# Four rows of a modulation made together in 32-column quarters of TensorE and spread over the partitions through DRAM

## The chip, the cores and the metric

The kernel runs on one core of a Trainium2 chip. A core has TensorE (PE, matrix products from SBUF into PSUM), VectorE (DVE), ScalarE (ACT), GpSimd (POOL) and SyncE (SP, which here issues nearly all DMA transfers). Every engine works through its own list of instructions in order and waits for others through semaphores. The metric is the device time of one execution in microseconds, the median of several.

## The reference

A block of a network, forward and backward, on 2048 rows of 512 values in bf16; the hidden width F is 1792. A vector `c` makes six modulation rows; two sublayers follow, a spectral filter and an MLP with squared ReLU. The outputs are the block's result and the gradients by x, the filter's two parts, w1, b1, w2, b2, c and w_mod.

```python
mod = (_silu(c) @ w_mod).reshape(c.shape[0], 6, 1, -1)
sa, ca, ga, sb, cb, gb = (mod[:, 0].copy(), ..., mod[:, 5].copy())
h = _layernorm(x, axis=-1) * (1 + ca) + sa
x = x + ga * _A_ref(h, A_w_r, A_w_i)      # irfft2(rfft2(h) * (w_r + i w_i))
h = _layernorm(x, axis=-1) * (1 + cb) + sb
x = x + gb * _B_ref(h, B_w1, B_b1, B_w2, B_b2)   # relu(h w1 + b1)**2 w2 + b2
```

## The kernel before

The kernel is written out instruction by instruction, and then `set_order` puts each engine's instructions into the order of a table, `ORDER`: a list of positions for each of the five engines. Tiles and buffers are given out by pools; who waits for whom follows from the data.

The stage of this change is the start, some 55 us. Four things run in it side by side:

- x is loaded (`x_sb`), its rows get their statistics on DVE (`row_stats`), are normalized (`row_norm`, whose result also goes to `n_dram`), multiplied by 1 + ca (L833) and folded (`fold_u`, L277 and L278). On the folded rows PE does the first half of the two-dimensional transform (L313, L314, into `psA`).
- PE multiplies the incoming gradient (transposed, `gT`) with the transposed w2, scaled by 2 gb (`w2T`, L892): work that fills PE wherever the rest waits.
- DVE and ACT make tables of sines and cosines (L245 to L256 and others).
- The six modulation rows are made. `mod_row(j)` multiplies silu(c), repeated over all 128 columns (`scb`), with a 512 x 512 block of w_mod: four 128x512 matmuls (L772) into `mod_ps`, of which there is one buffer, with the same row on all partitions as the result. ACT or DVE copies it to `modb` (L774 to L778). Row 5 is also made as a column, by sixteen 128x1 matmuls (L787), since w2T is scaled by it. Row 0 goes to `srow` (L781, L782), is turned into columns by four matmuls with `pm` (L864, `sacol`), and adds a constant to the transform (L871, `dcrow`, L350). Rows 3 and 4 (sb and 1 + cb) are turned into columns by eight matmuls (L876) that read `modb`; the result `mcol` is used much later (L1039, L1041).

Then `spec_f23` begins, the second half of the transform: eight groups of `psB` matmuls on PE, each emptied by ACT into `AE` (L359). Its first `psB` needs all folded rows and `dcrow`; the mcol matmuls stand right behind it on PE.

In the end stage the gradient of w2 is made in 14 chunks of 128 rows of F (`grad_w2`, L1441). Each chunk needs a transposed load from `h_dram` (`hn`, issued on SP at L1257), sixteen 128x512 matmuls (for chunks 10 and 13 two halves of sixteen 128x256), a copy on ACT (L1442) and a store (L1443). Buffers `hn` are used again, so a load waits for the last matmul of an earlier chunk.

## Time and profile before

| | us |
|---|---|
| timed runs, three: median | 394.21 |
| their lowest and highest | 394.0 and 395.75 |
| the profiled execution's own span, first to last instruction | 398.0 |
| PE busy in it | 382.1 |
| DVE, ACT, POOL busy in it | 334.8, 303.2, 33.3 |

For the profiled execution no time is given but its span, which is 3.8 us above the median of the timed ones. Its mean granted TensorE clock is 0.990 of full speed. Busy times are sums over stages with different limits; each stage has to be looked at by itself.

### The profile page before, as it was taken

How to read it: one execution, taken by the hardware profiler on the slowest of the kernel's cores; microseconds unless marked ns; L12 is line 12 of the kernel's file. 1: busy time of each engine (PE TensorE's matmuls, PEld its weight loads, DVE VectorE, ACT ScalarE, POOL GpSimd, SP SyncE). 2: the span in 40 equal slices, each digit the busy share in tenths (PEclk: the TensorE clock that was granted, in tenths of full speed). 3: DMA queues.
4: the chain of work that ended last, by engine and by line, in shares of the span. 5: the costliest groups of instructions: out<-in, count | busy, mean ns of one | idle time of the engine just before them, and what ended most of it. 6: DMA issues, size and time to landing. Idle time of an engine off the chain costs nothing.

```text
span 398.0 us, 8415 instructions
## 1 busy us (share of the span) xinstructions
PE 382.1 (96%) x3042; PEld 202.4 (51%) x3042; DVE 334.8 (84%) x822; ACT 303.2 (76%) x605; POOL 33.3 (8%) x114
## 2 busy tenths in 40 slices
PE   8999999999999999999999999999999999999495
PEld 3555677544444444444444435457666664444244
DVE  8899959949986699969997999957999989998430
ACT  4787899899896499759976999277665589998441
POOL 9151001000000000000000000012300000002100
PEclk9999999999999999999999999999999999999979
DMA  8999799874589999578928696999979998999995
GB/s 258 362 222 293 230 209 252 209 280 63 195 228 197 256 259 253 128 191 183 257 81 210 167 245 180 270 245 371 296 221 262 215 325 173 221 208 243 249 259 189
DMA packets 133957, 91.06 MB, mean 229 GB/s; under 512 B 86842, under 2 KB 119868, under 8 KB 133660
## 3 DMA queue, kind: packets, MB, share of 16 engines
q1 hardware_dynamic: 132904, 88.09, 87.1%
q0 software_dynamic: 832, 2.36, 1.8%
q8 instruction: 24, 0.39, 0.4%
q14 instruction: 17, 0.14, 0.1%
q10 hardware_dynamic: 180, 0.07, 0.1%
HBM read 38.70 MB, written 33.19 MB: 181 GB/s over the span
## 4 chain that ended last, share of the span: by engine, by line
PE 74%; ACT 12%; DMA 5%; DVE 4%; POOL 2%; issue 1%; SPq 0%; ACTq 0%; POOLq 0%; DVEq 0%
PE og_1s L1096 12%; PE og_0s L1096 11%; PE mm_0s L1441 6%; PE mm_1s L1441 6%; PE mm_0s L1342 5%; PE mm_1s L1342 5%; PE mm_1s L1064 4%; PE mm_0s L1064 4%; PE pst L1064 3%; DMA hn_1s<-h_dram 3%; PE mm_0s L892 2%; DMA Xb<-xs_dram 2%; ACT AE L359 2%; PE mm_1s L892 2%; ACT gab L896 2%; ACT gab L1073 1%
## 5 line engine op out<-in xcount | busy, mean ns | idle before, releaser
L1342 PEld LDWEIGHTS <-h_sb 128*64 128x64 bf16 (+1 forms) x464 | 28.7, 109 | 15.9 <-issue 0.9
L1073 ACT ACTIVATE gab<-gab 128x512 bf16<-128x512 bf16 x56 | 35.0, 648 | 0.5 <-DVE gab L1071 0.5
L1096 PEld LDWEIGHTS <-gab 128*128 128x128 bf16 x224 | 21.5, 98 | 27.0 <-ACT gab L1073 1.9
L1064 PEld LDWEIGHTS <-w 128*128 128x128 bf16 x224 | 21.2, 98 | 25.7 <-issue 1.7
L1342 PE MATMUL mm_0s<-gab,h_sb 128*64 128x384 bf16 (+2 forms) x288 | 32.7, 345 | 0.0
L892 PEld LDWEIGHTS <-w2T 128*128 128x128 bf16 (+1 forms) x280 | 22.9, 102 | 18.5 <-issue 3.9
L1096 PE MATMUL og_0s<-w1T,gab 128*128 128x512 bf16 x112 | 27.4, 379 | 0.2 <-ACT G_0s L1109 0.2
L1096 PE MATMUL og_1s<-w1T,gab 128*128 128x512 bf16 x112 | 27.6, 379 | 0.0
L1441 PE MATMUL mm_0s<-g_sb,hn_1s 128*128 128x512 bf16 x64 | 16.8, 423 | 6.0 <-DMA hn_1s<-h_dram 6.0
L1342 PE MATMUL mm_1s<-gab,h_sb 128*64 128x512 bf16 (+2 forms) x176 | 22.4, 370 | 0.0
L1064 PE MATMUL mm_1s<-h2T,w 128*128 128x512 bf16 x84 | 21.9, 379 | 0.0
L1064 PE MATMUL mm_0s<-h2T,w 128*128 128x512 bf16 x80 | 21.2, 379 | 0.0
L359 ACT ACTIVATE AE<-psB 128x1024 bf16<-128x1024 f32 x16 | 17.2, 1078 | 0.7 <-PE psB L355 0.6
L896 ACT CAST gab<-mm_1s 128x512 bf16<-128x512 f32 x24 | 14.8, 615 | 2.3 <-PE mm_1s L892 2.2
L892 PE MATMUL mm_0s<-gT_0s,w2T 128*64 128x512 bf16 (+1 forms) x76 | 16.1, 380 | 0.2 <-DVE gab L894 0.2
L892 PE MATMUL mm_1s<-gT_0s,w2T 128*128 128x512 bf16 (+1 forms) x72 | 15.6, 379 | 0.1
L1064 PE MATMUL pst<-h2T,w 128*128 128x512 bf16 x60 | 15.6, 379 | 0.0
L892 PE MATMUL mm_1s<-gT_1s,w2T 128*128 128x512 bf16 (+1 forms) x68 | 14.9, 379 | 0.3 <-ACT gab L896 0.2
L892 PE MATMUL mm_0s<-gT_1s,w2T 128*128 128x512 bf16 (+1 forms) x64 | 15.1, 379 | 0.0
L1441 PEld LDWEIGHTS <-hn_1s 128*128 128x128 bf16 x64 | 6.8, 107 | 15.3 <-DMA hn_1s<-h_dram 6.2
L321 POOL MEMSET AE<- 128x4 bf16 x4 | 0.4, 110 | 162.4 <-PE mm_1s L1064 162.4
L1441 PE MATMUL mm_1s<-g_sb,hn_0s 128*128 128x512 bf16 (+1 forms) x64 | 13.7, 352 | 0.0
(650 smaller groups left out, 1064.3 us busy)
## 6 DMA issues: line engine op xcount, KB each, us to landing
w<-in_B_w_dram SPq DMA_DIRECT2D x2, 1792.0 KB, 10.4
Xb<-xs_dram SPq DMA_DIRECT2D x4, 514.0 KB, 7.9
Z<-wz_dram SPq DMA_DIRECT2D x4, 514.0 KB, 7.5
x_sb<-in_A_x_dram SPq DMA_DIRECT2D x4, 512.0 KB, 6.2
n_dram<-x_sb SPq DMA_DIRECT2D x4, 512.0 KB, 6.2
h_dram<-h2r SPq DMA_DIRECT2D x8, 256.0 KB, 2.4
h_sb<-h_dram SPq DMA_DIRECT2D x4, 512.0 KB, 5.4
g_sb<-in_grad_out_dram SPq DMA_DIRECT2D x2, 1024.0 KB
```

The costliest lines, as they stand in the source:

```text
L321: nc.gpsimd.memset(ae[:, :, :, 256:257], 0.0)
L359: nc.scalar.activation(dst, ps.rearrange("p r b (e f) -> p (r b) f e", e=2), AF.Copy, scale=EF_S)
L892: nc.tensor.matmul(ps[m], lhsT=w2T[:, dc, fc * P + m.start:fc * P + m.stop], rhs=gT[b][:, :, dc, :], start=(dc == 0), stop=(dc == 3), **pos)
L896: nc.scalar.copy(out=gaT[b][:, fc, :], in_=ps)
L1064: nc.tensor.matmul(ps, lhsT=w1[:, dc, (fc + i) * P:(fc + i + 1) * P], rhs=h2T[b][:, :, dc, :], start=(dc == 0), stop=(dc == 3))
L1073: nc.scalar.activation(gh[:, i, :], gh[:, i, :], AF.Copy, accum_out=gb1[:, b, fc + i:fc + i + 1])
L1096: nc.tensor.matmul(ps, lhsT=lhs(fc), rhs=rhs[:, fc, :], start=(fc == 0), stop=(fc == NFC - 1))
L1342: nc.tensor.matmul(blocks(ps[m], fb), lhsT=h2_sb[:, t, dc * P + m.start:dc * P + m.stop], rhs=gh_rows(t, fb), start=(t == 0), stop=(t == N ...
L1441: nc.tensor.matmul(ps[:, 0:w], lhsT=hns[fc][:, t, :], rhs=g_sb[:, t, c:c + w], start=(t == 0), stop=(t == NT - 1))
```

## The change

`mod_row` becomes `mod_rows`. For one row (j = 1) it does what was done before. For the four rows 2, 5, 4, 3 it gives each row a quarter of TensorE's columns: the weight is 32 columns of the repeated silu(c), the result 32 partitions of `mod_ps`. One ACT instruction copies all four with a bias `one4`, which is 1 on the partitions of row 4 and 0 elsewhere. One row of each quarter is stored to the new `mod_dram` (4 x 512 values, 4 KB), and a second DMA reads them back into `modb` on all 128 partitions (512 KB); `modb` has its rows in another order for that. `mod_cols` is the old form of row 5, and now also makes row 0, straight as columns. Where row 0 was reversed on the copy to `srow`, two of its columns are now reversed by a matmul with a mirrored identity (`flip`). The table `ORDER` is new for all engines; of its lines one is shown.

```diff
 ORDER = {
     "PE": (
-        "0-7 30 8-13 31 14-16 52-59 17-22 32-47 23-26 64-67 27 60-63 28 76-83 29 68-75 89-93 237-240 84-88 99-103 241-242 245-246 "
+        "0-1 3 5 2 4 6 8 7 30 9 11 13 10 15 12 17 14 16 31 19 21 32-47 18 56-59 52-55 20 22-23 64-67 60-63 24 26 25 76-83 27 "
...
+    mod_dram = dram.tile([4, D], BF16, name="mod_dram")
...
-    GA_B, GB_B, CA1_B, CB1_B, SB_B = range(5)
+    GA_B, GB_B, CB1_B, SB_B, CA1_B = range(5)
...
-    srow = gall[:, 1, :]
-
-    def mod_row(j):
+    one4 = constp.tile([P, 1], FP32, name="one4")
+    nc.gpsimd.memset(one4, 0.0)
+    nc.gpsimd.memset(one4[64:96, :], 1.0)
+
+    def mod_rows(*js):
         ps = psM.tile([P, D], FP32, name="mod_ps", bufs=1)
+        if len(js) == 1:
+            for dc in range(4):
+                nc.tensor.matmul(ps, lhsT=scb[:, dc, :], rhs=wmt[js[0] // 2][:, dc, (js[0] % 2) * D:(js[0] % 2 + 1) * D], start=(dc == 0), stop=(dc == 3))
+            nc.scalar.activation(modb[:, CA1_B, :], ps, AF.Identity, bias=K["onef"])
+            return
         for dc in range(4):
-            nc.tensor.matmul(ps, lhsT=scb[:, dc, :], rhs=wmt[j // 2][:, dc, (j % 2) * D:(j % 2 + 1) * D], start=(dc == 0), stop=(dc == 3))
...
+            for q, j in enumerate(js):
+                nc.tensor.matmul(ps[32 * q:32 * q + 32, :], lhsT=scb[:, dc, 32 * q:32 * q + 32], rhs=wmt[j // 2][:, dc, (j % 2) * D:(j % 2 + 1) * D],
+                                 start=(dc == 0), stop=(dc == 3), tile_position=(0, 32 * q))
+        row4 = gall[:, 1, :]
+        nc.scalar.activation(row4, ps, AF.Identity, bias=one4)
+        nc.sync.dma_start(mod_dram, row4[0:P:32, :])
+        nc.sync.dma_start(modb[:, 0:4, :], mod_dram[None, :, :].broadcast_to([P, 4, D]))
+
+    def mod_cols(j):
+        psc = psM.tile([P, 4], FP32, name="sm_ps", bufs=1)
+        for cc in range(4):
+            for dc in range(4):
+                a = (j % 2) * D + cc * P
+                w = wmt[j // 2][:, dc, a:a + P]
+                nc.tensor.matmul(psc[:, cc:cc + 1], lhsT=w, rhs=sc[:, dc:dc + 1], start=(dc == 0), stop=(dc == 3))
+        return psc
+
+    psc = mod_cols(5)
...
-    mod_row(1)
+    mod_rows(1)
...
-    for j in (0, 4, 3, 2, 5):
-        mod_row(j)
+    flip = p0.tile([P, P], BF16, name="flip")
+    nc.gpsimd.tensor_copy(flip, K["ident"][:, ::-1])
+    psc = mod_cols(0)
+    nc.vector.tensor_copy(sacol[:, 0, :], psc)
+    psc = psM.tile([P, 2], FP32, name="sm_ps", bufs=1)
+    nc.tensor.matmul(psc, lhsT=flip, rhs=sacol[:, 0, 1:4:2], start=True, stop=True)
+    nc.vector.tensor_copy(sacol[:, 0, 1:4:2], psc)
+    nc.vector.tensor_scalar(sacol[:, 1, :], sacol[:, 0, :], -1.0, None, op0=ALU.mult)
+    mod_rows(2, 5, 4, 3)
...
-    for i in range(4):
-        sr = srow[:, i * P:(i + 1) * P]
-        nc.tensor.matmul(psc[:, i, :], lhsT=sr, rhs=pm, start=True, stop=True)
-    nc.vector.tensor_copy(sacol[:, 0:2, :], psc[:, 0:4, :].rearrange("p i k -> p k i"))
```

What the new table does to the lists is seen at three places. The line numbers in rows of the changed kernel are its own: L788 is the quarter matmul, L792 and L793 the two DMAs, L895 the mcol matmuls (L876 before), L911 the w2 matmuls (L892), L848 the store to n_dram (L831), L871 the loads of Z (L854), L1276, L1460 and L1462 the `hn` load, the chunk's matmul and its store (L1257, L1441, L1443).

First, PE where modulation rows are made. Before, a row of four full matmuls (here row 5, in part) stands between first-stage matmuls, and the other rows stand at four more places:

```order
L314 LDWEIGHTS fold_u_1s
L314 MATMUL psA_0s<-TA,fold_u_1s 128x2x128
L772 LDWEIGHTS gab
L772 MATMUL mod_ps<-wm_2s,gab 128x512
L772 LDWEIGHTS gab
L772 MATMUL mod_ps<-wm_2s,gab 128x512
L772 LDWEIGHTS gab
L772 MATMUL mod_ps<-wm_2s,gab 128x512
L313 LDWEIGHTS fold_u_0s
L313 MATMUL psA_1s<-TA,fold_u_0s 128x2x128
```

In the changed kernel all sixteen quarter matmuls stand together, of which these are the first four (`wm_1s` and `wm_2s` are the blocks of w_mod for rows 2, 3 and 4, 5; `gab` holds the repeated silu(c)):

```order
L911 MATMUL mm_0s<-gT_1s,w2T 128x512
L788 LDWEIGHTS gab
L788 MATMUL mod_ps<-wm_1s,gab 32x512
L788 LDWEIGHTS gab
L788 MATMUL mod_ps<-wm_2s,gab 32x512
L788 LDWEIGHTS gab
L788 MATMUL mod_ps<-wm_2s,gab 32x512
L788 LDWEIGHTS gab
L788 MATMUL mod_ps<-wm_1s,gab 32x512
```

They are the 242nd to 257th of PE's matmuls; the first `psB` is the 330th, and the mcol matmuls stand from the 348th on.

Second, SP and PE along the way through DRAM. On SP the two new DMAs stand among loads of Z and stores of n_dram; what a row waits for is in brackets, and `DMAHW7_49` and the like are the landings of earlier DMAs (a DMA also waits for the one before it on its own of eight such marks):

```order
L1098 DMA wz_dram<-in_A_w_i_dram 32x7x257 [waits DMAHW5_49]
L871 DMA Z<-in_A_w_r_dram 64x2x257 [waits DMAHW6_49]
L792 DMA mod_dram<-gab 4x512 [waits DMAHW7_49,Activation_49]
L848 DMA n_dram<-x_sb 128x2x1024 [waits DMAHW0_49,DVE_49]
L848 DMA n_dram<-x_sb 128x2x1024 [waits DMAHW1_49]
L871 DMA Z<-in_A_w_i_dram 32x7x257 [waits DMAHW2_49]
L793 DMA modb<-mod_dram 128x2048 [waits DMAHW7_49,DMAHW3_49]
L871 DMA Z<-in_A_w_i_dram 32x7x257 [waits DMAHW4_49]
L848 DMA n_dram<-x_sb 128x2x1024 [waits DMAHW5_49,DVE_49]
```

and on PE the mcol matmuls, which before waited for copies of ACT and DVE, wait for the second of them:

```order
L355 MATMUL psB<-Cd,utcs 64x128
L895 LDWEIGHTS modb [waits DMAHW3_49]
L895 MATMUL sm_ps<-pm,modb 128x1
L895 LDWEIGHTS modb
L895 MATMUL sm_ps<-pm,modb 128x1
```

So the rows now leave PE, ACT, SP and two transfers behind them before PE goes on past `psB`.

Third, SP at the end, where the last four chunks' loads stand (chunk 10 is the first `hn` row in both, then 11, 12, 13). Before:

```order
L1257 DMA_TRANSPOSE hn_0s<-h_dram 128x16x128
L1334 DMA gxl_1s<-gx_dram 128x1024
L1257 DMA_TRANSPOSE hn_1s<-h_dram 128x16x128
L1443 DMA out_dram<-gw_2s 128x512
L1257 DMA_TRANSPOSE hn_2s<-h_dram 128x16x128
L481 DMA wmc_1s<-in_w_mod_dram 128x4x512
L1257 DMA_TRANSPOSE hn_3s<-h_dram 128x16x128
L1443 DMA out_dram<-gw_3s 128x512
L1443 DMA out_dram<-gw_4s 128x512
```

In the changed kernel, from the store of chunk 4 on (`gw_5s` and `gw_7s` are chunks 5 and 7):

```order
L1462 DMA out_dram<-gw_4s 128x512
L1334 DMA out_dram<-b4r_0s 1x512
L1462 DMA out_dram<-gw_5s 128x512
L1462 DMA out_dram<-gw_7s 128x512
L1276 DMA_TRANSPOSE hn_1s<-h_dram 128x16x128
L481 DMA wmc_1s<-in_w_mod_dram 128x4x512
L1276 DMA_TRANSPOSE hn_2s<-h_dram 128x16x128
L1276 DMA_TRANSPOSE hn_3s<-h_dram 128x16x128
L1353 DMA gxl_1s<-gx_dram 128x1024
```

The load of chunk 11 (`hn_1s`) has moved behind the stores of chunks 4, 5 and 7. PE takes the chunks in the order 5, 7, 6, 9, 8, 10 (first half), 11 in the changed kernel, with the last four of chunk 9 behind chunk 8; before it was 5, 6, 7, 8, 9, 10 (first half), 11.

## Rows read from the trace of the kernel before

**Rows 1.** The page: busy time, share of the span and instructions of each engine.

```profile
PE 382.1 (96%) x3042; PEld 202.4 (51%) x3042; DVE 334.8 (84%) x822; ACT 303.2 (76%) x605; POOL 33.3 (8%) x114
```

**Rows 2.** Table by stages: us, busy PE, PEld, DVE, ACT, POOL, clock, DMA.

```profile
36.00:55.00 19.00, 19.00 (x173) 11.90 (x172) 16.03 (x50) 16.04 (x28) 1.75 (x4) 1.00 0.93 228
55.00:75.00 20.00, 19.66 (x287) 13.49 (x283) 17.94 (x36) 19.27 (x34) 2.01 (x6) 1.00 0.89 237
```

**Rows 3.** The chain of work that ended last, 30 to 56: start, us, what.

```profile
43.38 0.86 PE mod_ps L772 x4
...
45.11 0.89 PE mod_ps L871 x16
46.11 0.11 PE psA_1s L314
...
50.34 0.23 PE psB L355 x4
...
51.01 0.29 PE sm_ps L876 x8
```

**Rows 4.** Timeline of DVE around the last fold: start, us, engine, line, what.

```profile
46.14 0.68 DVE L256 TENSOR_TENSOR LF<-lf_w_0s,lf_mk 128x256 bf16<-128x256 bf16 x3
...
47.08 0.41 DVE L278 TENSOR_TENSOR fold_u_1s<-h_1s 128x512 bf16<-128x512 bf16 x1
47.41 0.24 DVE L180 TENSOR_SCALAR Cf<-Cf,cf_f 128x128 bf16<-128x128 bf16 x1
```

**Rows 5.** Timeline of PE, the first matmul on the last fold.

```profile
47.57 0.27 PE L313 MATMUL psA_1s<-TA,fold_u_1s 128*128 128x256 bf16 x1
```

**Rows 6.** Waits of PE: line, waited for, us in total, times, longest.

```profile
PE mm_0s L1441 <- DMA hn_1s<-h_dram: 6.0, 1, 6.0
```

**Rows 7.** Timeline of SP's queue in the tail.

```profile
366.24 5.22 SPq L1257 DMA_TRANSPOSE hn_1s<-h_dram  x1
```

**Rows 8.** Timeline of PE in the tail.

```profile
371.03 1.36 PE L1441 MATMUL mm_1s<-g_sb,hn_0s 128*128 128x256 bf16 x11
378.36 5.97 PE L1441 MATMUL mm_0s<-g_sb,hn_1s 128*128 128x512 bf16 x16 [5.96 <-DMA hn_1s<-h_dram]
```

**Rows 9.** The chain of work in the tail.

```profile
384.33 3.45 PE mm_1s L1441 x16
```

**Rows 10.** Table by stages of 5 us in the tail, columns as above.

```profile
370.00:375.00 5.00, 2.40 (x17) 1.42 (x15) 3.99 (x10) 2.70 (x5) 1.60 (x3) 1.00 1.22 156
375.00:380.00 5.00, 1.64 (x4) 0.58 (x5) 0.00 (x0) 0.00 (x0) 0.00 (x0) 0.63 1.11 305
```

**Rows 11.** The chain of work, 149 to 152: matmuls with 32-column weights.

```profile
149.85 0.98 PE acc L959 x16
```

**Rows 12.** The chain of work, 9 to 12: row 5 made as columns.

```profile
10.52 0.38 PE sm_ps L787 x16
```

**Rows 13.** Lines 776 and 865: count, shortest, median and longest in ns, starts, forms.

```profile
L776 DVE TENSOR_SCALAR modb<-mod_ps x1: 682/682/682, 38.8 to 38.8; 128x512 bf16<-128x512 f32 x1
...
L865 DVE CAST sacol<-sm_ps x1: 167/167/167, 28.7 to 28.7; 128x8 bf16<-128x8 f32 x1
```

**Rows 14.** Line 778, the same columns.

```profile
L778 ACT CAST modb<-mod_ps x3: 585/585/585, 40.8 to 44.3; 128x512 bf16<-128x512 f32 x3
```

**Rows 15.** Line 831, the stores of n_dram, 512 KB each.

```profile
L831 SPq DMA_DIRECT2D n_dram<-x_sb x4: 360/372/383, 34.3 to 43.0; - x4
...
DMA to landing us min/median/max: 3.7/6.2/7.0
```

**Rows 16.** DMA issues: count, size, median us from issue to landing.

```profile
LF_dram<-LF SPq DMA_DIRECT2D x4, 256.0 KB, 4.0
...
out_dram<-gw_0s SPq DMA_DIRECT2D x2, 128.0 KB, 1.7
...
wz_dram<-in_A_w_i_dram SPq DMA_DIRECT2D x4, 112.4 KB, 7.8
```

**Rows 17.** The tile hn_1s: its loads' times from issue to landing.

```profile
DMA to landing us min/median/max: 7.2/9.6/12.1
```

15 lines of the change are left out of this document (removed), and 171 rows, old and new, of the table ORDER.

## The prediction, as it stood before the result was known

> **What bounds the kernel now.** I read the page first, then the waits of TensorE (PE), the table by stages, and the chain of work through the stage that the change rewrites. PE is busy for 382.1 of 398.0 us [rows 1], so matmuls that disappear are worth something only where no other engine takes PE's place. In the stretch where the modulation rows are made, PE is full: 19.00 of 19.00 us between 36 and 55, with VectorE (DVE) at 16.03 and ScalarE (ACT) at 16.04; in the stretch behind it, 55 to 75, ACT (19.27 of 20) stands close to PE (19.66) [rows 2]. The chain of work there runs over PE from matmul to matmul, the modulation's among them [rows 3]. So the stage's end, the first `psB`, comes when PE has worked off what stands ahead of it.
>
> DVE is close behind. The last fold of the folded rows is L278's, from 47.08, 0.41 long, so to 47.49 [rows 4]; PE takes up its first matmul on that tile at 47.57 [rows 5], with no wait recorded. PE and DVE arrive there together, and this decides how much of PE's saving passes.
>
> The largest wait of PE is at the other end: 6.0 us for `hn_1s`, once [rows 6]. That load is issued at 366.24 [rows 7], PE has work until 371.03 + 1.36 = 372.4 and goes on at 378.36 [rows 8]. The first sixteen matmuls behind the wait take 5.97 us [rows 8], the next sixteen 3.45 [rows 9]; in the five microseconds of the wait the granted clock is 0.63, where it is 1.00 ahead of it [rows 10]. Of the two levels, 2.4 and 1.2 GHz, that is the lower one for a part of it, after PE had stood idle.
>
> **The change, part by part.**
>
> *PE, rows made.* Removed are five rows (j = 0, 4, 3, 2, 5) of four 128x512 matmuls. Four such cost 0.86 us on the chain [rows 3]: 5 x 0.86 = 4.30 us less. Added are sixteen matmuls on 32 columns of TensorE each. Nothing in the modulation had this form, but L959 has: sixteen 128x512 matmuls with a 32-column weight, four different quarters in turn, take 0.98 us on the chain [rows 11]. The new ones come in the same pattern, so I take 0.98. The other bound is that quarters don't run side by side: 16 x 0.215 = 3.44. The four-column form of row 0 costs the same as that of row 5, sixteen 128x1 matmuls in 0.38 us [rows 12]. The four `pm` matmuls go, one `flip` matmul comes; both are smaller than the chain's rounding. Net: -4.30 + 0.98 + 0.38 = **-2.9 us** (bounds -2.9 and -0.5).
>
> *DVE, which must let this through.* Ahead of the last fold the new order has two L256 less (0.68 / 3 = 0.23 each), one Cf multiplication (0.24) [rows 4], the copy L776 (0.68) and L865 (0.17) [rows 13], and b1col (a small copy, as L865). Three small operations on `sacol` come, 0.17 each by L865. That is 0.46 + 0.24 + 0.68 + 0.17 + 0.17 - 0.51 = 1.2 us less. Behind the last fold PE now has seven L892 matmuls before `psB` where it had eight, 0.2 less. If DVE decides, `psB` comes 1.4 us earlier; if PE decides, 2.9. So 0 to 1.5 of PE's saving goes into a wait for folds. I take the middle, **+0.8**: both engines' lists are laid out anew and the trace favours neither.
>
> *ACT.* Three copies into `modb` of 0.58 [rows 14] and two of row 0 become one. ACT isn't what the stage waits for: 0.
>
> *The trip through DRAM.* The rows leave for `mod_dram`, come back into `modb` on all partitions, and PE needs them at the mcol matmuls right behind the first `psB`. The write waits for ACT, the read for the write's landing, and both waits are taken by SyncE's queue (SP), with loads of Z, stores of n_dram and a transposing load behind them. Those feed later stages; the price is a delay by as much as SP stands, some 4 to 6 us by the landings below, and I take 0.
>
> Cover: between the last quarter matmul and mcol, PE has 32 first-stage matmuls of 0.11, 23 L892 (0.215 each, as L772), the sixteen of L871 (0.89) and the first `psB` (50.34 to 51.01, 0.67) [rows 3]: 3.5 + 4.9 + 0.9 + 0.7 = 10.0 us, and 0.8 more with the wait for folds: 10.8.
> Trip: the copy 0.58 [rows 14], two issues of 0.37 [rows 15], so 1.3, and two landings. For the write (4 KB) the trace has no equal: the shortest store row is 1.7 us (128 KB), that of this stage 4.0 (LF_dram), the longest of a small write 7.8 (wz_dram) [rows 16]. For the read of 512 KB I take the 512 KB transfers of this very stage, 3.7 / 6.2 / 7.0 [rows 15]. Shortest 1.3 + 1.7 + 3.7 = 6.7; middle 1.3 + 4.0 + 6.2 = 11.5; longest 1.3 + 7.8 + 7.0 = 16.1. Against 10.8: no stall, **+0.7**, or 5.3. I take the middle, since the stage's own rows are the nearest.
>
> *The start.* The loads are put in another order, with the first part of w2 two places later, behind row 5's block of w_mod, which keeps its place. One issue is some 0.4 us [rows 15]; PE's first w2 matmuls need both loads. Taken as 0, up to 0.8 later.
>
> *The tail.* The load that PE waits for, chunk 11 of `hn`, was issued 372.4 - 366.2 = 6.2 us before PE wanted it, and such loads land after 7.2 / 9.6 / 12.1 us [rows 17]. Even the shortest is 1.0 us late. In the new order it stands right behind the store of chunk 7, and between chunk 7 and its own use PE has 48 matmuls of 0.215 (chunks 6, 9, 8), sixteen half-width ones (0.11 each, as the 256-column ones of [rows 3]) and small ones: 10.3 + 1.8 and some more, about 13 us, less 1 for the copy and issue. 12 us is as long as the longest landing, so that wait should go. I take the least it can have cost, **-1.0**.
>
> Sum: -2.9 + 0.8 + 0.7 - 1.0 = -2.4 us. Against the profiled span: 398.0 - 2.4 = 395.6. That execution is 3.8 us above the median of the three timed runs, 394.21, and its tail (6.0 of waiting, 5.97 - 3.45 = 2.5 of slow matmuls) can well hold that excess; against the median: **391.8 us**.
>
> **Rivals.**
>
> *The tail gives more.* If the timed runs wait as long as the median landing makes them, 9.6 - 6.2 = 3.4 go in place of 1.0: 389.4. At most 8.5 - 3.8 = 4.7 go: 388.1. For: the row of 6.0. Against: the DMA engines are full there (1.22 and 1.11 of their time) [rows 10], and another load may take this one's place.
>
> *Other engines swallow it.* DVE decides the fold (1.4 passes, and the trip is then covered) and the tail stays as it is: 392.8; with the start 0.8 later 393.6.
>
> *The trip keeps pace with its neighbours.* The small write is issued four places behind a 512 KB store of n_dram; if its completion comes no sooner than that store's, 6.2, the trip is 1.3 + 6.2 + 6.2 = 13.7, the stall 2.9, and the time 394.21 - 2.9 + 0.8 + 2.9 - 1.0 = 394.0: no change. For: DMA engines 0.93 busy in the stage [rows 2]. Against: a 128 KB store lands after 1.7 [rows 16]. The Trainium skill, "DMA: Bandwidth & Descriptors", section "Queues, rings and completion order", says that a transfer's semaphore increment lands only after every earlier write from that DMA engine, which is this rival's mechanism and speaks against the change; by that rule the result is this one. No row of before shows a small write behind a large one, so the trace decides neither way.
>
> *The trip is late and nothing else helps: slower.* Both landings at their longest: PE stands at mcol 5.3 us with `psB` and all of the next stage queued behind it, and the tail is as before: -2.9 + 0.8 + 5.3 = +3.2, 397.4. It passes +0.5% (1.97 us, about what a measurement of this kernel tells from no change) from a stall of 4.1, so from a trip of 14.9.
>
> **How the numbers follow.** Forecast 0.42 (390.2 to 393.0), larger tail 0.20 (388 to 390), swallowed 0.12 (392 to 395), neighbours' pace 0.13 (393 to 396), late trip 0.13 (396 to 398.5). The range 387.6 to 395.8 leaves out the late trip and the edges. Faster than 392.24: 0.34 of the forecast, the larger tail, 0.04 of the swallowed: 0.58. Slower than 396.18: 0.13. Same: 0.29.
>
> **What would show it.** Sixteen quarter matmuls in about 1 us, and the first `psB` 1.4 to 2.9 us earlier against the first w2 matmul. At the mcol matmuls a wait of PE for `modb` of under 1 us; 3 or more speaks for the neighbours' pace. PE waiting for folds up to 1.5 us in all. No wait for chunk 11 in the tail, and a clock of 1.00 there. I am wrong if quarters run one after the other, if the trip is late, or if in the tail PE waits for another chunk.

## The result, and the profile after

The changed kernel takes 399.77 us (median of 4 runs, 399.27 to 400.7) where the kernel before takes 394.32 (4 runs, 394.0 to 395.75): ratio 1.0136, 95% interval 1.0111 to 1.0161. In a later session (after_again) it took 400.29 (6 runs) where the kernel before took 396.25: ratio 1.0116 (1.0057 to 1.0175). 391.8 was forecast, with 387.6 to 395.8 as range: it is slower, where faster was forecast. Ratios leave disturbed runs out; the kernel before itself reaches from 393.1 to 403.7 in the sessions below, so small differences between sessions are not read.

The page of the changed kernel's profile (span 397.5 us, time 399.27) has, in the line of [rows 1]:

```profile
PE 380.6 (96%) x3051; PEld 205.4 (52%) x3051; DVE 336.4 (85%) x823; ACT 303.3 (76%) x601; POOL 34.4 (9%) x117
```

These totals don't show the loss: the span is as long as that of [rows 1], since that execution holds the wait of 6.0 us in its tail [rows 6], and 2.5 us of its PE time are the sixteen matmuls at the lower clock behind it. The waits that the changed kernel has in their place are in the table by stages (columns as in [rows 2]):

```profile
36.00:55.00 19.00, 18.76 (x203) 11.99 (x202) 14.51 (x50) 17.65 (x30) 1.56 (x4) 1.00 0.82 196
55.00:75.00 20.00, 18.96 (x290) 13.48 (x288) 19.32 (x41) 17.50 (x31) 2.49 (x6) 1.00 1.00 255
71.00:82.00 11.00, 8.95 (x195) 5.43 (x188) 8.12 (x16) 7.68 (x14) 0.00 (x0) 1.00 0.67 193
308.00:320.00 12.00, 9.81 (x222) 6.41 (x218) 11.63 (x24) 5.01 (x11) 0.00 (x0) 1.00 1.01 208
375.00:380.00 5.00, 4.95 (x25) 2.29 (x24) 3.30 (x7) 4.12 (x8) 0.91 (x2) 1.00 0.95 205
```

The kernel before, in two of these stretches:

```profile
71.00:82.00 11.00, 10.70 (x221) 6.48 (x221) 8.93 (x17) 9.06 (x17) 0.00 (x0) 1.00 0.79 179
308.00:320.00 12.00, 12.00 (x214) 7.41 (x207) 10.82 (x23) 6.53 (x14) 0.00 (x0) 1.00 1.07 240
```

PE is now idle for 2.05 us in the forward stage of `psG` (L385) and for 2.19 in the backward one, where it had 0.30 and none. In the tail, 375 to 380, it is busy at clock 1.00 where [rows 10] had 1.64 of 5.00 at 0.63.

**The start went as forecast.** Timeline of PE, the first and last quarter matmuls and what follows:

```profile
38.35 0.39 PE L788 MATMUL mod_ps<-wm_1s,gab 128*32 128x512 bf16 x1
...
39.01 0.38 PE L788 MATMUL mod_ps<-wm_1s,gab 128*32 128x512 bf16 x1
39.33 0.28 PE L313 MATMUL psA_1s<-TA,fold_u_0s 128*128 128x256 bf16 x1
...
46.62 0.27 PE L313 MATMUL psA_1s<-TA,fold_u_1s 128*128 128x256 bf16 x1
...
49.09 0.30 PE L355 MATMUL psB<-Cd,utcs 128*64 128x128 bf16 x4
...
49.77 0.35 PE L895 MATMUL sm_ps<-pm,modb 128*128 128x1 bf16 x8
```

Sixteen quarters from 38.35 to 39.33 are 0.98 us. The first `psB`, 50.3 before, is at 49.09, though PE's first w2 matmul is 1.3 later (16.02, not 14.7): against that matmul it comes 2.5 earlier (33.07 us behind it, 35.57 before). The last fold,

```profile
45.65 0.42 DVE L277 TENSOR_TENSOR fold_u_1s<-h_1s 128x512 bf16<-128x512 bf16 x1
```

ends at 46.07, 0.55 ahead of its first matmul, where [rows 4] and [rows 5] had the two together. And the trip, in SP's queue, with the landing of its read as the tile mod_dram has it:

```profile
40.65 0.62 SPq L792 DMA_DIRECT2D mod_dram<-gab  x1
...
43.30 1.16 SPq L793 DMA_DIRECT2D modb<-mod_dram  x1
```

```profile
DMA to landing us min/median/max: 6.2/6.2/6.2
```

From the last quarter's end (39.39) the rows are there at 43.30 + 6.2 = 49.5; PE uses them at 49.77 and waits for nothing.

**PE's waits** (line, waited for, us in total, times, longest):

```profile
PE mm_0s L1460 <- DMA hn_1s<-h_dram: 1.5, 1, 1.5
PE psG_2s L385 <- DVE utcs L389: 1.5, 3, 0.8
PE mm_1s L1460 <- ACT gw_4s L1461: 1.2, 1, 1.2
...
PE psG_0s L385 <- DVE utcs L389: 0.8, 1, 0.8
PE psG_1s L385 <- DVE utcs L389: 0.8, 1, 0.8
...
PE psG_1s L385 <- ACT utcs L391: 0.7, 1, 0.7
```

The 6.0 of [rows 6] are gone, and short waits at `psG` have come: six for copies out of `psG`, four of them (2.6 us) in the backward stage, and a seventh of 0.5 for DVE's `Z` in the forward one, in the rows left out.

**Where the time goes** is read from the same instruction in both traces. How much later the changed kernel's profiled execution is than that of before: first `psC` (L338) -1.4; first forward `psT` (L401) -0.3; last w1 matmul (L1083) -0.3; first gw1 matmul (L1361) +0.9; first gw2 matmul (L1460) +4.8 (+5.9 in a second profile, whose last w1 matmul is at +0.7). So 1.2 is lost in the forward `psG` stage and 5.1 between 232 us and the gw2 matmuls. In that part DVE forms the products with Z and X (L444 to L447). DVE's first and last of them, before:

```profile
270.37 0.70 DVE L444 TENSOR_TENSOR p<-Z,G_0s 128x1028 bf16<-128x1028 bf16 x1 [4.22 <-ACT G_0s L339]
...
317.96 0.42 DVE L447 TENSOR_TENSOR Xb<-p 128x514 bf16<-128x514 bf16 x1
```

and in the changed kernel, with the copy of the column sums ahead of them:

```profile
266.83 0.69 DVE L1257 CAST grow<-acc 128x512 bf16<-128x512 f32 x1 [2.19 <-PE acc L978]
...
272.97 0.70 DVE L445 TENSOR_TENSOR p<-Z,G_0s 128x1028 bf16<-128x1028 bf16 x1 [3.28 <-DMA Z<-wz_dram]
...
321.47 0.42 DVE L447 TENSOR_TENSOR Xb<-p 128x514 bf16<-128x514 bf16 x1
```

The products start 2.6 us later and end 3.5 later, and the first gw2 matmul follows 11.3 us behind their end (10.0 before). The table by stages over just these stretches, before and changed:

```profile
270.37:318.38 48.01, 47.35 (x691) 31.19 (x686) 46.59 (x108) 28.83 (x51) 5.87 (x11) 1.00 0.93 270
```

```profile
272.97:321.89 48.92, 45.63 (x665) 34.72 (x662) 48.07 (x110) 28.42 (x50) 6.70 (x15) 1.00 1.07 268
```

Before, PE is full there (47.35 of 48.01) and DVE has 1.4 to spare, 0.9 of it a wait for a load that other executions of this order don't have. In the changed kernel DVE is full (48.07 of 48.92) and PE waits. DVE itself is busy 1.5 us longer than before, with 110 instructions for 108, and in the stretch waits for another engine only once:

```profile
DVE utcs L389 <- PE psG_2s L385: 0.2, 1, 0.2
```

So the stretch is longer by DVE's own list, and PE's waits at `psG` are those of the engine that is not full there.

### The profile page after: what moved, and what is told of

The parts are those of the page before. It is cut to its first block, busy times and chain, and to the rows that moved or that the text cites. A ratio compares the mean times of both kernels' runs of the same rounds, so it can differ in the third digit from the quotient of the medians.

```text
span 397.5 us, 8406 instructions
## 1 busy us (share of the span) xinstructions
PE 380.6 (96%) x3051; PEld 205.4 (52%) x3051; DVE 336.4 (85%) x823; ACT 303.3 (76%) x601; POOL 34.4 (9%) x117
## 5 line engine op out<-in xcount | busy, mean ns | idle before, releaser
L1361 PEld LDWEIGHTS <-h_sb 128*64 128x64 bf16 (+1 forms) x464 | 33.8, 109 | 13.0 <-issue 0.8
L1083 PEld LDWEIGHTS <-w 128*128 128x128 bf16 x224 | 21.4, 98 | 26.6 <-issue 2.8
L1361 PE MATMUL mm_0s<-gab,h_sb 128*64 128x384 bf16 (+2 forms) x288 | 33.1, 345 | 0.0
L911 PEld LDWEIGHTS <-w2T 128*128 128x128 bf16 (+1 forms) x280 | 23.5, 102 | 17.7 <-issue 2.4
L1361 PE MATMUL mm_1s<-gab,h_sb 128*64 128x512 bf16 (+2 forms) x176 | 23.3, 370 | 0.4 <-ACT gmbc L490 0.4
L1083 PE MATMUL mm_1s<-h2T,w 128*128 128x512 bf16 x84 | 23.1, 379 | 0.4 <-ACT r_1s L1084 0.4
L1083 PE MATMUL mm_0s<-h2T,w 128*128 128x512 bf16 x80 | 21.5, 379 | 0.0
L1083 PE MATMUL pst<-h2T,w 128*128 128x512 bf16 x60 | 17.3, 379 | 0.1
L1460 PE MATMUL mm_0s<-g_sb,hn_1s 128*128 128x512 bf16 x64 | 15.1, 379 | 1.5 <-DMA hn_1s<-h_dram 1.5
L911 PE MATMUL mm_1s<-gT_0s,w2T 128*128 128x512 bf16 (+1 forms) x72 | 15.8, 379 | 0.1
L911 PE MATMUL mm_0s<-gT_0s,w2T 128*64 128x512 bf16 (+1 forms) x76 | 15.6, 380 | 0.2
L911 PE MATMUL mm_0s<-gT_1s,w2T 128*128 128x512 bf16 (+1 forms) x64 | 15.4, 379 | 0.3 <-DVE gab L913 0.2
L911 PE MATMUL mm_1s<-gT_1s,w2T 128*128 128x512 bf16 (+1 forms) x68 | 15.2, 380 | 0.4 <-ACT gab L915 0.2
L401 PEld LDWEIGHTS <-utcs 128*128 128x128 bf16 x128 | 10.4, 97 | 9.2 <-issue 1.6
L1460 PE MATMUL mm_1s<-g_sb,hn_0s 128*128 128x512 bf16 (+1 forms) x64 | 13.6, 352 | 0.1
```

The source lines that it names most:

```text
L401: nc.tensor.matmul(ps[:, P * i:P * i + P], lhsT=CS[:, i, t].rearrange("p a b -> p (a b)"), rhs=K["Cf"][:, i, :], start=True, stop=True)
L911: nc.tensor.matmul(ps[m], lhsT=w2T[:, dc, fc * P + m.start:fc * P + m.stop], rhs=gT[b][:, :, dc, :], start=(dc == 0), stop=(dc == 3), **pos)
L1083: nc.tensor.matmul(ps, lhsT=w1[:, dc, (fc + i) * P:(fc + i + 1) * P], rhs=h2T[b][:, :, dc, :], start=(dc == 0), stop=(dc == 3))
L1361: nc.tensor.matmul(blocks(ps[m], fb), lhsT=h2_sb[:, t, dc * P + m.start:dc * P + m.stop], rhs=gh_rows(t, fb), start=(t == 0), stop=(t == N ...
L1460: nc.tensor.matmul(ps[:, 0:w], lhsT=hns[fc][:, t, :], rhs=g_sb[:, t, c:c + w], start=(t == 0), stop=(t == NT - 1))
```

## The experiments

All kernels compute the whole result. A kernel is its `ORDER` table: the numbers are the places of instructions in the program's text. Where two orders are joined, all that an instruction of the first part needs on other engines is in the first part too. "gw2" below is how much later the first gw2 matmul is than in the profile of before; these starts carry up to 2 us of chance from the first w2 matmul, which is 0.3 to 2.3 us late in kernels with the new start. Counted from the last w1 matmul (some 231 us) that chance drops out, and profiles with the same order behind it mostly agree to 0.2 us. In us behind that matmul:

| | first product | end of the last | first gw2 |
|---|---|---|---|
| kernel before, first profile | 38.7 | 86.7 | 96.7 |
| its second profile, and old order there (three joined kernels) | 38.7 | 85.9 | 95.9 to 96.0 |
| new_rows_old_order | 39.0 | 86.2 | 96.4 |
| changed kernel, two profiles; start_old_rest_new | 41.5 to 41.6 | 90.4 to 90.5 | 101.8 to 101.9 |
| old_to_n2_rest_new | 38.9 | 88.9 | 100.5 |
| fast_acc_late | 40.6 | 87.9 | 98.0 |
| fast_psg_bare | 38.7 | 90.9 | 101.7 |
| fast_late_bare | 40.6 | 92.8 | 104.0 |
| after_acc_early | 41.4 | 95.1 | 106.4 |
| after_acc_z_early | 41.4 | 91.5 | 102.8 |
| after_psg_filled | 40.1 | 92.2 | 102.4 |
| after_both_back | 41.4 | 94.8 | 105.2 |

The three joined kernels are start_new_rest_old, old_then_new_tail and new_start_old_middle_new_tail, each described below.

**Which part of the order.** The kernel before once more:

> The kernel before, unchanged, for a second profile. The profile that the prediction used had a span of 398.0 us, as long as that of the changed kernel (397.5), although the timed runs differ by 5 us. If that profile was an outlier in its tail alone, this one shows a span near 392.5, the same first psB (50.3 us), the same start of the w2 gradient (328.4) and a wait for chunk 11 of 1 to 4 us in place of 6.0. If the timed runs hide something else, the starts of the stages differ too.

397.27 us (span 395.2, not near 392.5); gw2 -1.0, all starts up to the last w1 matmul -0.3. Its tail waits 4.3 us for one chunk and 2.0 for another, where the first profile had 6.0 for one: the tail's waits differ between executions.

The new rows alone, in the order of before:

```diff
 PE: order of before
-mod_row's matmuls at five places, pm
+mod_rows' sixteen quarters at one place, mod_cols(0), flip
```

> The new modulation code (quarters, trip through DRAM, row 0 as columns) in the order of before: its instructions stand where the old ones stood, all others keep before's order on every engine. Theory A (the edit gains what was predicted of it, and the new order of the later stages loses it): 391 to 394 us, ratio to before 0.990 to 1.000. Theory B (the edit itself costs, by the trip or by delayed loads of Z behind it): 397 us or more.

395.61 us, ratio 0.9973 (0.9933 to 1.0013); first `psB` -0.3, gw2 -0.4. PE waits for folds:

```profile
PE psA_0s L313 <- DVE fold_u_1s L277: 0.7, 1, 0.7
PE psA_1s L313 <- DVE fold_u_0s L277: 0.6, 1, 0.6
```

Against its own first w2 matmul the first `psB` is 0.6 earlier: in the old order the folds take most of PE's saving, and the edit itself is no loss.

The new order to the mcol matmuls, then that of before; and the reverse:

```diff
-PE 3051, ACT 513, DVE 767, POOL 113, SP 299 entries: new order
+PE 355, ACT 58, DVE 181, POOL 73, SP 34 entries: new order; the rest: order of before
```

> The changed kernel whose order is the new one up to the mcol matmuls (and what they need on the other engines) and before's for all the rest. Theory A: 391 to 394 us, about 1 us less than before, as the new start's psB is 1.1 us earlier. Theory B (the start costs later, by what it delays): 397 us or more.

400.12 us (twelve runs, 394.3 to 404.1), ratio 1.0031 (0.9984 to 1.0078). First `psB` -2.1, first `psC` -0.7, since PE waits 1.2 for ACT's copy `gab` at the seam; gw2 -1.4. By its median this is theory B's 397 or more; but up to gw2 nothing is lost, as theory A has it, and in the profile the time goes in the tail, whose wait for a chunk is 8.4 us.

```diff
-PE 3051, ACT 513, DVE 767, POOL 113, SP 299 entries: new order
+PE 356, ACT 58, DVE 185, POOL 74, SP 39 entries: order of before; the rest: new order
```

> The reverse: the new modulation code in before's order up to the mcol matmuls, and the new order for all the rest. Theory A (the loss is in the later order): 398 to 401 us. Theory B: 391 to 395 us.

402.21 us, ratio 1.0169 (1.0123 to 1.0214); gw2 +6.5. The loss is in the order behind the start.

The tail by itself, from the first gw2 matmul:

```diff
-PE 3051, ACT 513, DVE 767, POOL 113, SP 299 entries: new order
+PE 2700, ACT 425, DVE 659, POOL 102, SP 219 entries: new order; the rest: order of before
```

> The changed kernel with its own order up to the first gw2 matmul (PE's list up to there, and whatever that needs on the other engines) and the order of before behind it. Theory A (the changed kernel loses its time between the forward products and the first gw2 matmul, and wins some back in its tail): the first gw2 matmul stays some 4.8 us later than before, the wait of PE for a chunk of hn in the tail comes back (3 to 8 us), and the time lies at 400 to 406. Rival B (the new order of the tail is what costs): the time falls below 398, towards before.

404.37 us, ratio 1.0194 (1.014 to 1.0248); gw2 +7.0. The wait for a chunk is back, at 3.0 us. But gw2 is later here than in the changed kernel, 104.6 against 101.8 behind the last w1 matmul, though the order up to there is the same: the old tail sets twelve `psT` matmuls ahead of it, and PE waits 1.6 for ACT's copies `Tsb` there. So the 2.3 us between 1.0194 and 1.0136 can be this seam, and the run doesn't show what the new tail is worth.

```diff
-PE 3051, ACT 513, DVE 767, POOL 113, SP 299 entries: new order
+PE 2783, ACT 454, DVE 704, POOL 104, SP 238 entries: order of before; the rest: new order
```

> The new modulation rows in the order of before up to about the first gw2 matmul, then the new order of the tail. Theory A: the first gw2 matmul stands where it stood before (0 to 0.6 us earlier), no wait of PE over 2 us for a chunk of hn in the tail, and the time is 390.5 to 393.5, below before. Rival B (the new tail costs, or the load of chunk 11 is late in any order): a wait of 3 us or more for some chunk stays, and the time is 395 or more.

394.17 us, ratio 0.9941 (0.9903 to 0.9979); gw2 -1.1, longest wait for a chunk 1.6. Faster than the kernel before, as theory A has it, though less than its 390.5 to 393.5. Against the new rows in the old order (0.9973) it is 1.3 us, with overlapping intervals.

New start, old middle, new tail:

```diff
-PE 3051, ACT 513, DVE 767, POOL 113, SP 299 entries: new order
+PE to 355: new order; PE to 2783: order of before; the rest: new order (other engines as in the two above)
```

> The new order up to the mcol matmuls, that of before from there to about the first gw2 matmul, and the new order of the tail. Theory A: psB 1 to 2 us earlier than before, the first gw2 matmul 0.5 to 1.5 us earlier, no long wait in the tail, and 390 to 393: the fastest of all. Rival C (what the start wins is lost at the seam or swallowed by the engines behind it, as ACT did where only the start was new): as the old order with the new tail, within 0.5 us.

394.09 us, ratio 0.9953 (0.9914 to 0.9991), the profiled run 392.53; first `psB` -2.1, first `psC` -0.7, gw2 -1.4. Rival C holds: 1.4 of the start's 2.1 are gone at the seam. With the old middle the new rows and the new tail are faster than the kernel before; with the new middle they are slower.

**Ahead of 232 us or behind it.** Both joins fall at the end of the forward products:

```diff
-PE 3051, ACT 513, DVE 767, POOL 113, SP 299 entries: new order
+PE 1618, ACT 331, DVE 506, POOL 81, SP 148 entries: new order; the rest: order of before
```

> The new order up to the first w1 matmul and, on all engines, all that hangs on those instructions (PE's list up to some 230 us), then the order of before. Theory A1 (the loss is made behind the forward products, in the order of the backward stages from 231 to 333 us): the first gw2 matmul within 1 us of before, and the time as before's with its tail, 394 to 398. Rival A2 (the loss is seeded in the forward part, where PE waits in 71 to 82): the first gw2 matmul 2 us or more later, and 398 to 402.

405.39 us, ratio 1.0207 (1.0144 to 1.0269). Last w1 matmul +0.8, first gw1 +7.5, gw2 +7.1: neither theory's number, because the seam itself waits (PE 2.0 for ACT's `utcs` and 1.8 for DVE's `v_2s`, both at L304). It tells only that ahead of the seam nothing near 5 us was lost.

```diff
-PE 3051, ACT 513, DVE 767, POOL 113, SP 299 entries: new order
+PE 1629, ACT 331, DVE 512, POOL 82, SP 152 entries: order of before; the rest: new order
```

> The new rows in the order of before up to the end of the forward products (PE's list to some 232 us, and what hangs on it on the other engines), then the new order for all the rest, the backward stages and the tail. Theory A1 (most of the loss is made behind 232 us): the first gw2 matmul 3.5 to 6 us later than before, 398.5 to 401 us. Rival A2 (the loss is seeded in the forward part): the first gw2 matmul at most 1 us later than before, 393 to 396 us.

399.08 us, ratio 1.0085 (1.0049 to 1.0121); last w1 -0.4, gw2 +3.4, so 3.8 us are lost behind 232 us in an execution that had the old order up to there. Theory A1. Here the products start as early as before (38.9 behind the last w1 matmul against 38.7), and gw2 is still 4.5 later than with the old order (100.5 against 95.9): their stretch is 2.8 longer, and gw2 follows 1.6 later behind it. So most of the loss does not need a late start of the products:

```profile
270.16:320.18 50.02, 46.99 (x692) 35.88 (x688) 48.16 (x110) 29.64 (x52) 6.81 (x14) 1.00 1.06 263
```

**The late sums.** In the changed kernel the last sixteen `acc` matmuls (column sums, 32-column weights) stand behind the first `psB` of the backward pass, and the two `y_1s` products that they read behind the last folds. Before, they stand ahead, in two groups. SP's first load of Z waits for `acc`. Into the kernel with the old middle, this is put (530 and 549 are the products, 1793-1808 the sums; 1881, the matmul that spreads `grow`, has to move behind them):

```diff
 PE
-1717-1720 1706-1709 1793-1800 1849-1852 1749-1756 1853-1868 1801-1808 1757-1764 1869-1872 1881 1809-1824 1873-1880
+1717-1720 1706-1709 1849-1852 1749-1756 1853-1868 1757-1764 1869-1872 1809-1824 1793-1808 1873-1878 1881 1879-1880
 DVE
-538 530 540
-559 549 547-548 560
+538 540
+559 547-549 530 560
```

> The other way round: new_start_old_middle_new_tail, 394.1 us, and in it alone the last two y_1s products and the last sixteen acc matmuls moved to where the changed kernel has them (behind the last folds, and behind the first psB of the backward pass); SyncE's list is untouched, so its transposing load and what follows waits there with the Z load. Theory D: the first product 2 to 3.5 us later than in that kernel, the first gw2 matmul 1.5 to 3 us later, 395.5 to 397.5 us. Rival E: the first gw2 matmul within 0.5 us, 394.1 to 394.6.

397.24 us where that kernel has 394.09; ratio 1.0027 (1.0002 to 1.0053). DVE's first product, without and with the edit:

```profile
269.69 0.70 DVE L444 TENSOR_TENSOR p<-Z,G_0s 128x1028 bf16<-128x1028 bf16 x1 [4.22 <-ACT G_0s L339]
```

```profile
271.65 0.70 DVE L444 TENSOR_TENSOR p<-Z,G_0s 128x1028 bf16<-128x1028 bf16 x1 [4.51 <-ACT G_0s L339]
```

2.0 later, and the stretch of products is as long as before, 47.25 us:

```profile
269.69:316.94 47.25, 47.25 (x691) 31.09 (x686) 46.55 (x108) 28.63 (x51) 5.55 (x11) 1.00 0.93 271
```

```profile
271.65:318.90 47.25, 47.25 (x691) 31.09 (x686) 46.50 (x108) 28.64 (x51) 5.42 (x11) 1.00 0.93 257
```

gw2 goes from -1.4 to +0.6. So a late start of the products is passed on whole: 2.0 us, as theory D has it. What ends the wait is ACT's `G_0s` here, not Z; the later load of Z is not what cost the time in this kernel. It is ACT's own list: there `gmbc`, which needs the late sums, stands ahead of the first copy into `AE`,

```profile
265.79 0.58 ACT L490 CAST gmbc<-mm_1s 128x512 bf16<-128x512 f32 x1 [2.92 <-PE mm_1s L488]
266.27 1.03 ACT L359 ACTIVATE AE<-psB 128x1024 bf16<-128x1024 f32 x1
```

so that copy begins at 266.27 instead of 264.32. In the changed kernel `gmbc` stands behind two copies into `AE`. The 2.0 are thus not the changed kernel's: its first product waits for Z, 1.85 us past ACT's second `G_0s`. In the profile another 1 us is a longer wait of the tail (3.7 us for a chunk).

The other way round, the sums back to their old places in the changed kernel, and then also the load of Z (185) ahead of SP's transposing load (180):

```diff
 PE
-1765-1792 1753 1749 1754-1756 1750-1752 1849-1877 1761-1764 1878 1757-1760 1879-1880 1809-1824 1793-1808 1825-1840
+1765-1800 1753 1749 1754-1756 1750-1752 1849-1877 1801-1808 1761-1764 1878 1757-1760 1879-1880 1809-1840
 DVE
-538 550
-556-559 547-549 530 560
+538 530 550
+556-559 549 547-548 560
```

> The changed kernel with two places of its order taken back: the last two y_1s products on VectorE and the last sixteen acc matmuls on TensorE stand where they stood before (in two groups of eight, ahead of the last transposes), SyncE's list is untouched. Theory D (the acc matmuls, moved behind the first psB of the backward pass, hold up the first load of Z, and with it VectorE's products of 273 to 322 us, which VectorE works off without a pause): the last acc 2 to 3 us earlier, the first Z load only about 1 us earlier since two other transfers stand ahead of it on SyncE, the first product 0.5 to 1.0 earlier, the first gw2 matmul as much, 398.3 to 399.3 us. Rival E (the start of the products doesn't decide, the way gw1 is spread among the psG groups does): the first gw2 matmul within 0.3 us of the changed kernel's, 399.8.

```diff
 SP
-183 180 194 185
+183 185 180 194
```

> As after_acc_early, and the first Z load moved ahead of the transposing load and the LFb load on SyncE. Theory D: the first product 1.5 to 1.9 us earlier than in the changed kernel (then ScalarE's copy G_0s, which ends at 271.1 there, ends the wait), the first gw2 matmul 1.3 to 2 us earlier, 397.5 to 398.5 us. Rival E: the first gw2 matmul within 0.3 us and 399.8, or later, since the transposing load is now later.

403.09 us (ratio 1.0186, 1.0155 to 1.0217) and 402.16 (1.0161, 1.0121 to 1.0201): slower than the changed kernel, where theory D had up to 2 us gained. In the first the products start at 272.99 and the stretch is 53.71 us long; in the second they start at 271.71, the stretch is 50.14 instead of 48.92 and gw2 is at +4.8. But the second execution was 1.1 us ahead at the last w1 matmul already: counted from there the products start in both only 0.2 earlier than in the changed kernel (41.4 for 41.6), and gw2 comes 4.6 and 1.0 later. Put back, the sums stand ahead of the first backward `psB`, which comes 1.6 later (35.4 for 33.7 behind the last w1 matmul), and ACT's copies with it. In the second they now end DVE's wait:

```profile
271.71 0.70 DVE L445 TENSOR_TENSOR p<-Z,G_0s 128x1028 bf16<-128x1028 bf16 x1 [1.46 <-ACT G_0s L339]
```

So their return alone gains nothing, since other work has been fitted round them; and as the start hardly moved, the two runs don't test theory D in the changed kernel.

**The psG groups.** Between the first and the last of the 192 backward `psG` matmuls the old order has 79 gw1 matmuls spread over five gaps; the changed kernel has 41 in two, and at the end 108 `psG` matmuls in a row:

```profile
316.01 0.40 PE L385 MATMUL psG_0s<-LGb,Z 64*128 64x128 bf16 x12
317.20 0.41 PE L385 MATMUL psG_0s<-LGb,Z 64*128 64x128 bf16 x12 [0.79 <-DVE utcs L389]
...
318.87 0.41 PE L385 MATMUL psG_2s<-LGb,Z 64*128 64x128 bf16 x12 [0.80 <-DVE utcs L389]
...
320.40 0.41 PE L385 MATMUL psG_1s<-LGb,Z 64*128 64x128 bf16 x12 [0.67 <-ACT utcs L391]
...
320.97 2.61 PE L1361 MATMUL mm_0s<-gab,h_sb 128*128 128x384 bf16 x15
```

That spacing, put into the kernel with the old middle (2422 to 2613 are `psG`, the others gw1). The second gap holds 41 gw1 matmuls here, where the changed kernel has 32 (its 41 are both gaps together):

```diff
 PE
-2422-2433 2470-2481 2446-2457 2350-2365 2320-2325 2434-2445 2458-2469 2482-2493 2366-2381 2494-2505 2542-2553 2518-2529
-2390-2421 2530-2541 2506-2517 2622-2628 2566-2577 2590-2601 2554-2565 2629-2630 2578-2589 2602-2613
+2350-2365 2320-2325 2366-2372 2422-2433 2470-2481 2373-2381 2446-2457 2434-2445 2458-2469 2482-2505 2390-2421 2622-2630
+2542-2553 2518-2541 2506-2517 2566-2577 2590-2601 2554-2565 2578-2589 2602-2613
```

> new_start_old_middle_new_tail, 394.1 us, and in it alone the 79 gw1 matmuls that stand between the first and the last psG group of the backward pass put where the changed kernel has them: 29 ahead of the first group, 9 behind 24 psG matmuls, 41 behind 84, and the last 108 psG matmuls in a row with nothing between. Theory F (in that row PE has nothing to do while VectorE and ScalarE copy psG away): 1.5 to 3 us of waits of PE at psG, the first gw2 matmul 1.5 to 3 us later, 395.5 to 397.5. Rival (VectorE's products set the pace of that stage in any case, and gw1 done earlier is time won back behind it): psG waits, but the first gw2 matmul within 0.5 us, 394 to 394.6.

398.94 us, ratio 1.006 (1.0027 to 1.0092); gw2 +5.9, and 5.7 later than in that kernel counted from the last w1 matmul. PE waits 3.7 us at `psG` in that stage, more than theory F's 1.5 to 3. But DVE's waits show another cause beside the bare row:

```profile
DVE utcs L389 <- PE psG_1s L385: 5.5, 2, 3.0
```

DVE's own order still has its copies of `psG` at the old places; where PE does 41 gw1 matmuls first, DVE stands for 5.5 us with the products queued behind the copy, and these take 52.16 us instead of 47.25. DVE's busy time in the stretch stays that of its old list, 46.6 us, where the new list has 48.1. In the changed kernel DVE's longest wait of this kind is 0.2. So the run shows that PE's spacing and DVE's list belong together, and not that the bare row is what the changed kernel pays.

Both edits, the late sums and the bare row:

```diff
 PE, DVE
+the edit of fast_acc_late
+the edit of fast_psg_bare
```

> Both edits at once: the sums late (as fast_acc_late, 397.2) and the psG groups in a row (as fast_psg_bare), all else as in new_start_old_middle_new_tail. If the two make up the loss of the changed kernel's backward stages, the first gw2 matmul comes 4 to 5 us later than in that kernel and the time is 398.3 to 400. If they are the same wait seen twice, it is as late as with the worse of the two alone, 396.5 to 397.7.

400.14 us, ratio 1.0091 (1.0058 to 1.0123); products from 272.81 to 324.97 (the 52.16 of the bare row, begun later), gw2 +7.8. Counted from the last w1 matmul gw2 is 8.1 later than in the kernel without them, where 4 to 5 were expected and the two alone give 2.0 and 5.7: they are separate costs and add up, both with waits that the changed kernel doesn't have, of ACT for `gmbc` and of DVE for `psG`.

In the changed kernel, sixteen of the gw1 matmuls behind the row (2622 to 2637) put into it, with one of ScalarE's copies moved (the other stood there already):

```diff
 PE
-2494-2517 2530-2577 2590-2613 2578-2589 2622-2636 2618 2637 2619-2621
+2494-2517 2622-2626 2530-2553 2627-2631 2554-2577 2590-2601 2632-2637 2602-2613 2578-2589 2618-2621
 ACT
-402 411 414 405 412
+402 411 405 414 412
```

> The changed kernel, and in it alone the sixteen gw1 matmuls that follow the last psG matmul of the backward pass put between the last nine psG groups (5, 5 and 6 of them, where PE waits 0.79, 0.80 and 0.67 us), and ScalarE's two copies of gw1 sums ahead of the utcs copies that they stood behind. Theory F: the waits at psG fall from 3.3 to about 1 us in that stretch, the first gw2 matmul 1 to 2.3 us earlier, 397.5 to 398.8. Rival (the 5.0 us in which VectorE then waits for gs_0s decide): the first gw2 matmul within 0.4 us, 399.4 to 400.2.

400.94 us, ratio 1.0116 (1.0066 to 1.0167), the ratio that the changed kernel had in its later session. The waits at `psG` fall from 2.6 us to 1.1 there, but PE waits 1.1 for ACT's copy `gw_2s` and 0.9 at `psT` instead, and the products end later (52.18 us long). gw2 +5.9, 0.6 later than in the changed kernel from the last w1 matmul. Theory F's gain does not come. But DVE's list was left as it was, and DVE now waits 2.2 us for `psG_2s`, so the waits have moved rather than gone.

Both taken back at once, with the `sel` matmul (1881) ahead of the first `psB`; the changed kernel itself beside it:

```diff
 PE, ACT, DVE, SP
+the edits of after_acc_z_early and after_psg_filled
-1906-1910 1881 1845
-1809-1824
+1906-1910 1845
+1881 1809-1824
```

> The changed kernel with both arrangements taken back at once: the last sixteen acc matmuls, the y_1s products, the first Z load and now the sel matmul on grow (L488) too as they stood before, and sixteen gw1 matmuls between the last nine psG groups as in after_psg_filled. If the two arrangements are what the backward stages lost and only held each other up when taken back singly, the first gw2 matmul comes 2.5 to 5 us earlier than in the changed kernel and the time is 395 to 397.5. If the loss belongs to the whole order (the copies of psB, psC and gw1 on ScalarE, the gw1 matmuls done too early), the first gw2 matmul stays within 1 us and the time at 398.8 to 401.

> The changed kernel as it is, on the same chip as after_both_back. By its first four runs 399.3 to 400.7; the ratio to the kernel before 1.008 to 1.014, by how often that one's tail waits long on this chip.

402.34 us, ratio 1.0163 (1.0102 to 1.0223), against 400.29 for the changed kernel. Counted from the last w1 matmul the products start 0.2 earlier than in the changed kernel, take 53.39 us, and gw2 is 3.4 later; `psB` is 1.6 later again. The loss belongs to the order of these stages as a whole: these two places of it can't be given back alone.

## Why the prediction was wrong

**The step that failed** is what the sum left out. It ends at the first `psB` and begins again in the tail; the 300 us between them stand in it at nothing, though the diff says that `ORDER` is new for all engines, and the three places that were laid side by side are none of them there. The only word on later stages is that of SP's delayed loads, "and I take 0". The runs place the loss: between 232 us and the first gw2 matmul 5.1 us of the changed kernel against the first profile of before, 5.8 against the old order at its usual length, 3.8 and 4.5 even where the order up to there is the old one (old_to_n2_rest_new), and none with the old order in that stretch (old_then_new_tail, new_start_old_middle_new_tail).

How those us come about is worked out from the stretch of the products, counted from the last w1 matmul. Against the kernel with the old middle, gw2 is 101.8 - 96.0 = 5.8 us later: the products start 2.9 later, take 48.92 - 47.25 = 1.7 longer, and gw2 follows 11.3 instead of 10.0 behind them, 1.3. In six kernels with the old middle the stretch is 47.25 us with PE busy throughout (47.24 and 48.01 in the two profiles of before): the old order keeps PE and DVE full together. The new one has DVE full (48.07 of 48.92) and PE waiting.

The 1.7 go with DVE's list: its busy time in the stretch is 46.5 to 46.6 us in every kernel with the old list, whatever PE does, and 48.1 to 48.5 in those with the new one. The 2.9 are read from the trace: ACT's second `G_0s` is 1.0 later, and the load of Z, which in the new order waits for the late sums, lands another 1.85 behind it. How late the start is varies with that landing (40.1 in after_psg_filled, 38.9 in old_to_n2_rest_new), and old_to_n2_rest_new loses 4.5 of the 5.8 with an early one, so it is not the main cost. The 1.3 behind the products has a row: PE does fifteen gw1 matmuls (2.61 us, from 320.97) ahead of the first backward `psT`, which stands 1.5 us behind the products' end in the changed kernel (323.42) and 0.3 before (318.72). Where these are moved into the row of `psG` (after_psg_filled, after_both_back), gw2 follows 10.1 and 10.5 behind the products, but the stretch pays for it. What in DVE's new list makes its 1.5 us, and which list would give the whole loss back, stays open.

**PE, rows made: right.** Quarters run side by side, 0.98 us for sixteen, as L959 let expect.

**DVE lets through +0.8: right, by order.** In the new order PE waits for no fold, and 2.5 of the 2.9 come through (`psB` against the first w2 matmul, 1.4 to 2.9 said), so the term was 0.4. In the old order PE waits 1.3 us for folds and 0.6 comes through, as the rival "other engines swallow it" has it.

**The trip, +0.7: too dear, on the safe side.** It took 10.1 us, not 11.5, and PE got there 0.3 after it, with no wait. The write landed within 43.30 - 40.65 = 2.65 us, where 4.0 was taken. The rival "neighbours' pace" did not come, for a reason that it overlooked: the queue waits in order. SP's issue before the write ends at 34.97, then SP stands until ACT's copy is done at 40.63, and meanwhile the transfers ahead run out. The busy tenths of the DMA engines from 36 to 46, in slices of 0.25 us:

```profile
DMA  9999952000000000000000000899999999989899
```

The write finds them empty. The Trainium skill, "DMA: Bandwidth & Descriptors", section "Queues, rings and completion order", lets a semaphore increment land only after every earlier write from that DMA engine; no large write was in flight ahead of this one, so the trace doesn't test the rule.

**The start, 0: too low.** It cost 1.3 us in this execution and 0.3 to 2.3 in others with this start; the bound had been 0.8. Four matmuls of row 1 and one more now stand ahead of the first w2 matmul:

```profile
14.94 0.81 PE L783 MATMUL mod_ps<-wm_0s,gab 128*128 128x512 bf16 x3
15.58 0.38 PE L759 MATMUL mm_0s<-ones_sq 128*128 128x512 bf16 x1
15.80 0.38 PE L783 MATMUL mod_ps<-wm_0s,gab 128*128 128x512 bf16 x1
16.02 1.04 PE L911 MATMUL mm_0s<-gT_0s,w2T 128*128 128x512 bf16 x4
```

They are not the reason: the same five stand there in new_start_old_middle_new_tail, whose first w2 matmul is at 14.98, 0.3 later than before. What differs is further ahead: in the changed kernel's profile the `ones_sq` matmuls (L759) stand some 0.43 us apart until 8.8 us, in that one 0.22 from 6.7 us on, with a granted clock of 1.00 in both. Why stays open.

**What the start wins is not kept.** That was no term at all. From `psC` (-1.4) to `psT` (-0.3) the forward `psG` stage takes back 1.2, with PE idle 2.05 of 11 us, most of it waits for DVE (0.8, 0.5 and 0.3 us at `psG`); with the old order behind the start 1.4 of 2.1 go at a wait for ACT instead. Stretch 55 to 75 was named as one where ACT stands close to PE [rows 2], and this wasn't carried to the sum: a lead of PE's is worth there what DVE and ACT let through.

**The tail, -1.0: right in sign, its size not settled.** From the first gw2 matmul to the end it takes 64.1 to 70.8 us in the six profiles with the old tail and 62.1 to 67.7 in the thirteen with the new one. By ratios the new tail gives 1.3 us in the old order (0.9941 against 0.9973), less than their intervals leave open. Chunk 11 no longer waits: its load, issued at 373.39, lands at 379.31 and is used at 381.69. That was in part luck: 8.3 us lie between issue and use, where 12 were forecast, since the copy and the store of chunk 7 came late, and the longest landing of [rows 17], 12.1, would have been too late; this one took 5.9. And PE waits for another chunk, which the prediction had named as a sign of being wrong: 1.5 us for chunk 5, at 356.94, and in the changed kernel's second profile 4.1, with the sixteen-matmul row behind it slow:

```profile
360.61 6.27 PE L1460 MATMUL mm_0s<-g_sb,hn_1s 128*128 128x512 bf16 x15 [4.07 <-DMA hn_1s<-h_dram]
```

The sum also sets a span beside times: all through the record an execution's time is 1.7 to 2.2 us above its span (399.27 and 397.5 here), so the profiled execution of before was nearer 6 than 3.8 us above the median, and of its 8.5 us in the tail less than the rival's 4.7 was left to win.

The late trip, the rival on the slower side, did not happen; the time went to its side by a mechanism that no rival named.
